# An attention and two-MLP kernel: two weight blocks are multiplied after the last attention products, and the sums for the second half of the tokens are made during the last two blocks of the first half

## The chip, the cores and the metric

The kernel runs on one core of one Trainium2 chip. A core has five engines that run their own instruction lists side by side: TensorE (PE in the profile, with its weight loads as PEld), VectorE (DVE), ScalarE (ACT), GpSimd (POOL) and SyncE (SP), which issues the DMA transfers. The metric is the time of one execution in microseconds (us); lower is better. A difference under about 0.3% (2.9 us here) can't be told from no change.

## The reference, cut to what matters

```python
def attention(q, k, v):                    # 4 batches x 8 heads x 576 positions x 64
    scores = (q @ k.T) / 8
    # heads 0-3 see the last 32 positions; heads 4-7 every 32nd earlier position
    p = softmax(where(mask, scores, -1e9))
    return p @ v
x = attention(q, k, v)                     # brought to 2304 tokens x 512
xn = x / sqrt(mean(x * x) + 1e-6) * rms_g
g = silu(xn @ w_gate) * (xn @ w_val)       # 512 -> 1536
x = g @ w_out                              # 1536 -> 512
x = softplus(x @ w_in) @ w_out2            # 512 -> 2048 -> 512
```

The weights arrive as 64-bit floats. The kernel turns them into 32-bit floats on the chip: one ScalarE and three VectorE instructions for each 128x512 piece (`decode`, L267).

## The kernel before, in words

**Precision.** Every matrix product of the MLPs is made of three products (`mm3`, L332; the matmul is L338): a number is split into a high part and a low part (ScalarE makes the high one; VectorE at L260 or GpSimd at L262 subtracts it to get the low one), and hi x hi, hi x lo and lo x hi are added in PSUM. The tile `win` holds split weights, `ob` and `tb` split activations, `gh`/`gl` the split hidden values, `xs` the activations.

**Tokens.** The 2304 tokens are cut into five chunks (512, 512, 512, 512, 256). Chunks 0 and 1 are side one (tokens 0 to 1023; batches 0 and 1 are tokens 0 to 1151), chunks 2, 3 and 4 are side two. The hidden width 1536 of the first MLP is cut into twelve blocks of 128, f = 0 to 11. A product of one block's gate or value rows with one 512-token chunk takes 12 matmuls; the text calls such a product a half (of the pair gate, value).

**Three stages, each planned as a whole.** The class `Program` (L49) records instructions and, at each `emit`, lists each engine's work in the order of a simulated schedule. TensorE has two streams (main work, and fillers marked `side`, which are taken where they can begin first); the other engines take what is ready by due times. Within an engine the order is fixed from then on.

1. *Attention of batches 0 and 1* (16 units; scores, mask, exponential, transposes, values), with fillers dealt to unit numbers by `at_step` (L861 to L869): weights of f = 0 and 1, the RMS statistics (`stats`, L344), normalising and splitting of chunk 0 at unit 13 and of chunk 1 at unit 20, that is after the last, and `half` and `glu` of f = 0 and 1 for chunk 0 from unit 14 to 19. `glu` loads ScalarE's silu table and then the exponential's again.
2. *Side one* of the first MLP, f = 0 to 11, with the attention of batches 2 and 3 dealt in, three items a pass; the items are used up at f = 9. Low parts of the hidden values (`chain1`, L724) are made on VectorE.
3. *The rest*: the remaining output products of side one (`drain`), `build` for side two, the first MLP on side two, then the second MLP on both sides.

**Side two and sums.** For two whole chunks `quad` makes a 2x2 block product with seven products in place of eight. It needs four sums of activations, T1 to T4, each split into high and low. `build` (L788) makes these and the plain splits at the start of side two, before the products that read them. `quad`'s results are put together with a ScalarE copy (L680) and a VectorE add (`plus`, L684). `early2` decodes weights of the second MLP, three pieces in each of the first blocks of side two.

**Output sums.** `out1` (first MLP) and `out2` (second) take PSUM into `xs`: the first block pair by a VectorE copy (L763, L781), the others by a VectorE add (L765, L783).

## Time and profile before

| | us |
|---|---|
| median of 3 runs | 967.75 (965.78 to 968.31) |
| profiled execution | 966.85 |
| its span in the trace | 964.8 |
| around the span | 2.05 |
| PE busy | 907.4 (94%) |
| DVE busy | 748.3 (78%) |
| ACT busy | 473.4 (49%) |
| POOL busy | 208.4 (22%) |

The profile is read by stretches of the span. Attention of batches 0 and 1 ends near 84 us, side one runs to 325 us, the first MLP on side two starts there. PE's busy share is near full in most stretches, and the granted clock stands beside it: at 0.50 TensorE runs at 1.2 GHz, at 1.00 at 2.4 GHz. A row of the timeline merges neighbouring instructions of one line; "[3.73 <-POOL ssq L566]" means that the engine had been idle for 3.73 us and was released by GpSimd's write of `ssq` at L566.

### The profile page before, as it was taken

The page shows a single profiled execution, that of the slowest core. Times are in us where ns is not written, and L with a number is a line of the kernel's source. Part 1 is how long each engine was busy: PE and PEld are TensorE (multiplying, and loading weights), DVE is VectorE, ACT ScalarE, POOL GpSimd, SP SyncE. Part 2 cuts the span into 40 slices and gives each one's busy share as a digit, 9 for nine tenths or more (in the row PEclk, how much of TensorE's full clock was granted, in tenths as well). Part 3 has the DMA queues.
Part 4 walks back from the last instruction along what each step waited for, and adds up shares of the span by engine and source line. Part 5 has one row for each costly group of instructions (what it writes and reads, how often), then busy time and mean ns, then how long its engine had stood idle before and what let it go on. Part 6 is the DMA issues. An engine that isn't in the chain of part 4 may idle for free.

```text
span 964.8 us, 14035 instructions
## 1 busy us (share of the span) xinstructions
PE 907.4 (94%) x5244; PEld 746.1 (77%) x5244; DVE 748.3 (78%) x1238; ACT 473.4 (49%) x883; POOL 208.4 (22%) x185
## 2 busy tenths in 40 slices
PE   6785999999999789999999988999999999999998
PEld 6663777777878667888888877888876888888886
DVE  6774879897943998999899997777779676666654
ACT  5576555556451545544445455444455544344331
POOL 2454111140222654332234161000013000000000
PEclk7777999999999889999999999999999999999999
DMA  9920966756420025545554422111120411101002
GB/s 196 257 76 25 280 201 188 228 135 189 140 88 1 22 88 153 175 142 176 164 168 149 151 68 55 55 45 48 53 65 22 153 40 38 44 23 44 22 1 109
DMA packets 42035, 103.11 MB, mean 107 GB/s; under 512 B 5040, under 2 KB 5744, under 8 KB 41968
## 3 DMA queue, kind: packets, MB, share of 16 engines
q1 hardware_dynamic: 41968, 102.23, 35.8%
q8 instruction: 41, 0.67, 0.3%
q14 instruction: 26, 0.21, 0.1%
HBM read 79.66 MB, written 22.54 MB: 106 GB/s over the span
## 4 chain that ended last, share of the span: by engine, by line
PE 46%; DVE 9%; DMA 2%; issue 2%; ACT 1%; POOL 0%; SPq 0%; ACTq 0%; DVEq 0%
PE bank L338 46%; DVE w L260 2%; DMA w<-w_kept 1%; DVE xs L765 1%; DVE xs L260 1%; DMA w_kept<-cvtx 1%; DVE cvu L277 1%; DVE win L260 1%; DVE cvu L275 1%; DVE gv L684 1%; DVE cvtx L280 0%; DVE gv L732 0%; ACT cvtx L274 0%; DVE gvx L684 0%; DVE tb L260 0%
## 5 line engine op out<-in xcount | busy, mean ns | idle before, releaser
L338 PE MATMUL bank<-ob,win 128*128 128x512 f32 (+1 forms) x1560 | 340.2, 364 | 10.8 <-ACT ob L255 5.2
L338 PEld LDWEIGHTS bank<-ob,win 128*128 128x128 f32 x1560 | 267.9, 192 | 62.3 <-ACT ob L255 6.7
L338 PE MATMUL bank<-tb,win 128*128 128x512 f32 x672 | 175.5, 396 | 13.6 <-ACT gv L680 5.8
L338 PEld LDWEIGHTS bank<-tb,win 128*128 128x128 f32 x672 | 126.0, 191 | 43.0 <-ACT gv L680 6.8
L783 DVE TENSOR_TENSOR xs<-bank,xs 128x512 f32<-128x512 f32 x126 | 86.5, 688 | 52.9 <-PE bank L338 52.5
L309 ACT ACTIVATE win<-w 128x512 fp32r<-128x512 f32 (+1 forms) x136 | 83.0, 614 | 86.9 <-DVE w L260 31.9
L338 PE MATMUL bank<-wout,ghx 128*128 128x512 f32 x304 | 94.1, 391 | 0.6 <-DVE xs L783 0.6
L260 DVE TENSOR_TENSOR win<-w,win 128x512 fp32r<-128x512 f32 x112 | 78.7, 703 | 19.7 <-ACT win L309 19.4
L338 PE MATMUL bank<-ghx,wout 128*128 128x512 f32 x224 | 84.9, 399 | 0.0
L338 PE MATMUL bank<-gh,wout 128*128 128x512 f32 (+1 forms) x256 | 81.8, 355 | 3.2 <-DVE xs L765 2.1
L338 PE MATMUL bank<-wout,gh 128*128 128x512 f32 x272 | 84.0, 390 | 0.0
L765 DVE TENSOR_TENSOR xs<-bank,xs 128x512 f32<-128x512 f32 (+1 forms) x100 | 62.3, 629 | 14.5 <-PE bank L338 14.1
L260 DVE TENSOR_TENSOR w<-w 128x256 f32<-128x256 f32 x112 | 71.1, 635 | 2.0
L338 PEld LDWEIGHTS bank<-wout,ghx 128*128 128x128 f32 x304 | 56.6, 188 | 13.3 <-DVE xs L783 1.9
L338 PE MATMUL bank<-wout,glx 128*128 128x512 f32 x152 | 59.3, 390 | 0.3 <-DVE glx L260 0.3
L338 PEld LDWEIGHTS bank<-wout,gh 128*128 128x128 f32 x272 | 50.8, 188 | 10.8 <-DVE xs L783 0.4
L338 PEld LDWEIGHTS bank<-gh,wout 128*128 128x128 f32 x256 | 45.8, 189 | 11.0 <-DVE xs L765 2.7
L277 DVE SCALAR_TENSOR_TENSOR cvu<-raw,cvu 128x512 uint32<-128x512 uint32 x68 | 52.3, 769 | 1.3
L338 PE MATMUL bank<-wout,gl 128*128 128x512 f32 x136 | 52.9, 389 | 0.0
L338 PEld LDWEIGHTS bank<-ghx,wout 128*128 128x128 f32 x224 | 42.1, 188 | 9.4 <-DVE xs L765 0.4
L720 ACT ACTIVATE gh<-gvx 128x512 fp32r<-128x512 f32 (+1 forms) x38 | 21.3, 561 | 56.0 <-PE bank L338 33.9
L338 PE MATMUL bank<-gl,wout 128*128 128x512 f32 (+1 forms) x128 | 44.9, 351 | 1.7 <-POOL gl L262 1.7
(153 smaller groups left out, 1381.8 us busy)
## 6 DMA issues: line engine op xcount, KB each, us to landing
raw<-w SPq DMA_DIRECT2D x68, 512.0 KB, 4.4
w<-w_kept SPq DMA_DIRECT2D x56, 256.0 KB, 2.6
w_kept<-cvtx SPq DMA_DIRECT2D x27, 256.0 KB, 4.4
cvt<-w_kept SPq DMA_DIRECT2D x27, 256.0 KB, 2.8
w_kept<-w SPq DMA_DIRECT2D x24, 256.0 KB, 3.9
out<-xs SPq DMA_DIRECT2D x18, 256.0 KB, 2.0
w_kept<-cvt SPq DMA_DIRECT2D x17, 256.0 KB, 4.6
cvtx<-w_kept SPq DMA_DIRECT2D x17, 256.0 KB, 3.0
```

The lines of the kernel that those rows point to most:

```text
L260: dve(n, lambda: getattr(nc.vector, name)(o, x, y), r, w)
L275: dve(512, lambda: nc.vector.tensor_scalar(out=u, in0=t.bitcast(U32), scalar1=0x80000000, scalar2=None, op0=ALU.bitwise_and), [kt], [ku], ...
L277: dve(512, lambda: nc.vector.scalar_tensor_tensor(out=u, in0=wlo, scalar=29, in1=u, op0=ALU.logical_shift_right, op1=ALU.bitwise_or), [kra ...
L309: act(n, lambda: nc.scalar.activation(h, t, AF.Copy), [kt], [reg(0, o + lo, o + hi)])
L338: lambda a=a, b=b, i=i, st=st, mv=mv: nc.tensor.matmul(o, lhsT=st[a], rhs=mv[b], start=(first and i == 0), stop=(last and i == m - 1), ski ...
L684: dve(CH, lambda: nc.vector.tensor_add(o[0], y[0], o[0]), [y[1], o[1]], [o[1]])
L720: act(n, lambda: nc.scalar.activation(h, src, AF.Copy), [ksrc], [kh])
L765: dve(n, lambda: nc.vector.tensor_add(x, pb, x), [kp, kx], [kx])
L783: dve(DM, lambda: nc.vector.tensor_add(x, pb, x), [kp, kx], [kx])
```

## The change

1. Chunk 1's statistics, normalising and splitting leave the fillers and come after attention, as do both `glu` of f = 0 and 1, which now share one silu table. The halves of f = 0 and 1 for chunk 0 go to fillers 18 and 19. The loads of their weights are planned behind the key loads of units 12 and 14 (`hold`). Chunk 1's low parts are all made on VectorE.
2. `sq`, which holds squares for the statistics, has two buffers in stage one.
3. The first `out1` and `out2` of a sum, copies out of PSUM, go from VectorE to ScalarE: 20 in the first MLP, 18 in the second.
4. f = 10 and 11 of side one go from stage two's plan to stage three's. There the low parts of their hidden values are made on GpSimd, and `combine`, the part of `build` that makes T1 to T4, stands behind f = 10. It writes its sums into the `gv` buffers, since chunks 2 and 3 are still read. `build` at the start of side two is left with the plain splits.
5. `early2`: two pieces a block for twelve blocks (24), and 8 more beside the second MLP's side one; before, three a block until 32 were made.

```diff
+DEALT = 10
-START = (13, 20)
+START = 14
+HOLD = (12, 14)
...
-        dma(512, lambda: nc.sync.dma_start(out=raw, in_=src), [], [kraw])
+        dma(512, lambda: nc.sync.dma_start(out=raw, in_=src), hold, [kraw])
...
-        sq = ring(at, "sq" + tag, 1, [128, 6 * SK])
+        sq = ring(at, "sq" + tag, nsq, [128, 6 * SK])
...
         if first:
-            dve(n, lambda: nc.vector.tensor_copy(x, pb), [kp], [kx])
+            act(n, lambda: nc.scalar.activation(x, pb, AF.Copy), [kp], [kx])
...
-    def build(c0, c1, c4, direct=True):
+    def combine(c0, c1, over):
         for k in (0, 1):
             (b11, k11), (b12, k12), (b21, k21), (b22, k22) = xv(k, c0), xv(k, c1), xv(k + 2, c0), xv(k + 2, c1)
-            if direct:
-                split_op(b11, k11, B11, k, eng="DVE")
-                split_op(b21, k21, B21, k, eng="DVE")
-                split_op(b22, k22, B22, k, eng="POOL")
             t, kt = fk["gv"].next()
             sub("DVE", CH, t, b12, b11, [k12, k11], [kt])
             split_op(t, kt, T1, k, eng="POOL")
             sub("POOL", CH, b12, b22, b12, [k22, k12], [k12])
             split_op(b12, k12, T3, k, eng="POOL")
-            two("DVE", CH, "tensor_add", b11, b12, b11, [k12, k11], [k11])
-            split_op(b11, k11, T2, k, eng="DVE")
-            sub("DVE", CH, b21, b21, b11, [k21, k11], [k21])
-            split_op(b21, k21, T4, k, eng="DVE")
+            t, kt = (b11, k11) if over else fk["gv"].next()
+            two("DVE", CH, "tensor_add", t, b12, b11, [k12, k11], [kt])
+            split_op(t, kt, T2, k, eng="DVE")
+            y, ky = (b21, k21) if over else fk["gv"].next()
+            sub("DVE", CH, y, b21, t, [k21, kt], [ky])
+            split_op(y, ky, T4, k, eng="DVE")
+    def build(c0, c1, c4, sums=True):
+        for k in (0, 1):
+            for kk, c, slot, eng in ((k, c0, B11, "DVE"), (k + 2, c0, B21, "DVE"), (k + 2, c1, B22, "POOL")):
+                x, kx = xv(kk, c)
+                split_op(x, kx, slot, k, eng=eng)
+        if sums:
+            combine(c0, c1, True)
...
-                split_op(x, kx, slots[kk // 2], kk % 2, eng="DVE" if kk % 2 else "POOL")
+                split_op(x, kx, slots[kk // 2], kk % 2, eng="DVE" if kk % 2 or c and kk < 3 else "POOL")
...
-        at_step(4, prep1, 0, 0)
-        at_step(9, prep1, 1, 0, (0,))
-        for c, u in enumerate(START):
-            at_step(u, stats, c, f_banks)
-            at_step(u, direct, c)
-        for f, u in ((0, START[0] + 1), (1, START[0] + 4)):
-            at_step(u, half, f, 0)
-            at_step(u + 1, half, f, 1)
-            at_step(u + 2, glu, f)
+        at_step(16, prepare, 0, (0, 1), HOLD[0])
+        at_step(17, prepare, 1, (0,), HOLD[1])
+        at_step(START, stats, 0, f_banks)
+        at_step(START, direct, 0)
+        for f, r_ in ((0, f_banks), (1, s_banks)):
+            for row in (0, 1):
+                at_step(18 + f, half, f, row, r_)
...
+            stats(1, t_banks)
+            direct(1)
+            table("silu_and_others")
+            for f in (0, 1):
+                g[f, 0] = chain1(gates[f, 0], gates[f, 1])
             pr.emit()
...
-            for f in range(W1N):
+            for f in range(DEALT):
+                side_a(f, queue)
             step(queue, len(queue))
             pr.emit(start=0)
...
+        for f in range(DEALT, W1N):
+            side_a(f, [])
+            if f == DEALT:
+                combine(*SIDES[1][:2], False)
         drain(len(todo))
-        build(*SIDES[1])
+        o_banks.t = banks.t[4:]
+        build(*SIDES[1], False)
...
-            for k in range(3 * f, min(3 * f + 3, 2 * W2N)):
-                early2(k)
+            early2(2 * f)
+            early2(2 * f + 1)
```

`side_a(f, queue)` is the loop body of stage two under a name: weights, gate and value products, `chain1` (its low parts on VectorE for f below 10, on GpSimd from there), and the output products to drain.

**TensorE at the end of stage one.** Rows of the order before: L526 are value products (`vb_105` of units 12 and 13, `vb_106` of the last two), L502 transposes, L338 halves, and L352, a few rows further on, the statistics of chunk 1.

```order
69 L338 MATMUL bank_76<-ob,win_89 128x512 x12
70 L338 MATMUL bank_77<-ob,win_89 128x512 x5
71 L526 MATMUL bank_75<-pt_115,vb_105 64x64 x6
72 L338 MATMUL bank_77<-ob,win_89 128x512 x2
73 L526 MATMUL bank_75<-pt_116,vb_105 64x64 x2
74 L502 MATMUL bank_72<-id_sb,pp_114 128x128 x3
75 L502 MATMUL bank_73<-id_sb,pp_114 128x128 x3
76 L338 MATMUL bank_77<-ob,win_89 128x512 x5
77 L338 MATMUL bank_76<-ob,win_89 128x512 x2
78 L526 MATMUL bank_74<-pt_117,vb_106 64x54 x6
```

The same place now; lines L530, L506, L342 and L356 are what L526, L502, L338 and L352 were.

```order
67 L530 MATMUL bank_75<-pt_115,vb_105 64x64 x6
68 L530 MATMUL bank_75<-pt_116,vb_105 64x64 x2
69 L342 MATMUL bank_77<-ob,win_89 128x512 x12
70 L342 MATMUL bank_76<-ob,win_89 128x512 x12
71 L342 MATMUL bank_70<-ob,win_89 128x512 x3
72 L506 MATMUL bank_72<-id_sb,pp_114 128x128 x3
73 L506 MATMUL bank_73<-id_sb,pp_114 128x128 x3
74 L342 MATMUL bank_70<-ob,win_89 128x512 x2
75 L530 MATMUL bank_74<-pt_117,vb_106 64x54 x6
76 L530 MATMUL bank_74<-pt_118,vb_106 64x54 x6
77 L530 MATMUL bank_75<-pt_117,vb_106 64x54 x6
78 L530 MATMUL bank_75<-pt_118,vb_106 64x54 x4
```

The value products of unit 13 (rows 67 and 68) stand ahead of 27 matmuls of halves now; before, 17 and more stood ahead of them. Between the last transposes and the value products of the last units stand two matmuls of halves, and none between those products; before, seven stood ahead of them and seven more between them.

**VectorE between stage two and stage three.** Before: L260 are low parts of weights (`win`) and of hidden values (`glx`), L356 to L359 the statistics of chunks 3 and 4, L765 output sums.

```order
396 L260 TENSOR_TENSOR win_89<-w_82,win_89 128x512
397 L732 TENSOR_TENSOR gvx_916<-bank_77,gvx_916 128x512
398 L260 TENSOR_TENSOR win_89<-w_82,win_89 128x512
399 L260 TENSOR_TENSOR glx_923<-gvx_916,ghx_920 128x512
400 L356 SCALAR_TENSOR_TENSOR gvx_917<-bank_73,ssq_b 128x512
401 L356 SCALAR_TENSOR_TENSOR gv_83<-bank_72,ssq_b 128x256
402 L358 TENSOR_TENSOR gvx_917<-gvx_917,ssq_b 128x512
403 L358 TENSOR_TENSOR gv_83<-gv_83,ssq_b 128x256
404 L359 SCALAR_TENSOR_TENSOR ssq_b<-gvx_917,ssq_b 128x512
```

Now: L360 to L363 are the statistics, L279, L281 and L284 a decode of weights of f = 10, L262 low parts and sums.

```order
372 L362 TENSOR_TENSOR gv_83<-gv_83,ssq_b 128x256
373 L363 SCALAR_TENSOR_TENSOR ssq_b<-gvx_915,ssq_b 128x512
374 L363 SCALAR_TENSOR_TENSOR ssq_b<-gv_83,ssq_b 128x256
375 L279 TENSOR_SCALAR cvu_81<-w_82 128x512
376 L281 SCALAR_TENSOR_TENSOR cvu_81<-raw_78,cvu_81 128x512
377 L262 TENSOR_TENSOR gvx_915<-xs 128x512
378 L284 SCALAR_TENSOR_TENSOR w_82<-w_82,cvu_81 128x512
379 L279 TENSOR_SCALAR cvu_81<-w_82 128x512
380 L281 SCALAR_TENSOR_TENSOR cvu_81<-raw_79,cvu_81 128x512
381 L262 TENSOR_TENSOR win_89<-w_82,win_89 128x512
```

Before, the weights of f = 10 are decoded and split (rows 396 and 398 end it) ahead of the statistics of chunks 3 and 4; now their decode stands behind them, with `combine`'s first sum (377) in its middle. On TensorE the gate product of f = 10 follows the products of these statistics directly in both orders.

## Rows read from the trace of the kernel before

**Rows 1.** The page: the chain that ended last, by engine.
```profile
PE 46%; DVE 9%; DMA 2%; issue 2%; ACT 1%; POOL 0%; SPq 0%; ACTq 0%; DVEq 0%
```
**Rows 2.** Windows: stretch, length, busy time (instructions) of each engine; columns in row one.
```profile
core 0: us, PE busy (x) PEld busy (x) DVE busy (x) ACT busy (x) POOL busy (x), PEclk, DMA share, GB/s
282.00:325.00 43.00, 43.00 (x192) 35.56 (x191) 22.50 (x34) 14.21 (x27) 12.65 (x11) 1.00 0.02 7
325.00:374.00 49.00, 38.67 (x173) 30.90 (x172) 47.62 (x60) 25.32 (x47) 30.59 (x22) 0.90 0.28 86
336.00:340.00 4.00, 4.00 (x15) 3.20 (x15) 4.00 (x5) 2.13 (x4) 4.00 (x4) 0.61 0.01 2
440.00:560.00 120.00, 118.90 (x630) 102.38 (x629) 112.37 (x181) 59.20 (x108) 36.49 (x29) 1.00 0.49 156
...
600.00:620.00 20.00, 20.00 (x89) 16.55 (x89) 15.45 (x26) 9.74 (x18) 0.00 (x0) 1.00 0.22 62
```
**Rows 3.** Timeline, end of stage one: start, busy, engine, line, operation, [idle before <-releaser].
```profile
42.51 1.87 PE L445 MATMUL bank<-kl,ql 128*64 128x96 f32 x20 [2.23 <-DVE eb L458]
...
66.42 1.32 POOL L485 TENSOR_TENSOR pp<-eb,mz 128x324 f32<-128x324 f32 x2 [1.27 <-DVE mz L476]
66.69 6.09 PE L338 MATMUL bank<-ob,win 128*128 128x512 f32 x20
...
74.14 0.87 PE L502 MATMUL bank<-id_sb,pp 128*128 128x128 f32 x6
...
79.12 1.28 ACT L198 ACT_TABLE_LOAD   x1
79.23 0.79 PE L526 MATMUL bank<-pt,vb 54*64 54x54 f32 x20
...
82.67 1.26 POOL L262 TENSOR_TENSOR gl<-gv,gh 128x512 fp32r<-128x512 f32 x1
...
84.64 2.08 PE L352 MATMUL bank<-ssq,ones 128*128 128x512 f32 x2 [3.73 <-POOL ssq L566]
```
**Rows 4.** VectorE by line, 36 to 49 us: count | busy us, mean ns | idle before.
```profile
L277 DVE SCALAR_TENSOR_TENSOR cvu<-raw,cvu 128x512 uint32<-128x512 uint32 x2 | 2.0, 1024 | 0.0
L280 DVE SCALAR_TENSOR_TENSOR w<-w,cvu 128x512 uint32<-128x512 uint32 x2 | 1.9, 956 | 0.0
L260 DVE TENSOR_TENSOR win<-w,win 128x512 fp32r<-128x512 f32 x2 | 1.8, 883 | 0.0
```
**Rows 5.** Timeline, the statistics of chunks 3 and 4.
```profile
280.50 1.56 PE L352 MATMUL bank<-ssq_b,ones 128*128 128x512 f32 x4 [0.64 <-POOL ssq_b L566]
...
281.70 3.10 PE L338 MATMUL bank<-ob,win 128*128 128x512 f32 x12
...
283.73 1.28 ACT L198 ACT_TABLE_LOAD   x1
...
286.12 8.45 POOL L262 TENSOR_TENSOR xs<-xs,ssq_b 128x512 f32<-128x512 f32 x8 [5.68 <-DVE ssq_b L359]
...
286.81 0.87 DVE L359 SCALAR_TENSOR_TENSOR ssq_b<-gv,ssq_b 128x256 f32<-128x256 f32 x1
```
**Rows 6.** Waits of PE, 325 to 380 us: total, times, longest.
```profile
PE bank L338 <- POOL tb L262: 4.2, 1, 4.2
```
**Rows 7.** Timeline, PE and DVE, the start of side two.
```profile
325.44 1.52 PE L338 MATMUL bank<-ob,win 128*128 128x512 f32 x6
...
333.89 1.76 DVE L260 TENSOR_TENSOR ob<-xs,ob 128x512 fp32r<-128x512 f32 x1
335.58 0.68 DVE L765 TENSOR_TENSOR xs<-bank,xs 128x512 f32<-128x512 f32 x1
...
370.88 1.52 PE L338 MATMUL bank<-tb,win 128*128 128x512 f32 x6
372.24 1.59 PE L338 MATMUL bank<-ob,win 128*128 128x256 f32 x12
372.57 0.68 DVE L684 TENSOR_TENSOR gvx<-bank,gvx 128x512 f32<-128x512 f32 x1
```

More of the change, by code (lines that the diff above doesn't have):

```diff
@@ L265, in sub @@
         two(eng, n, "tensor_sub", o, x, y, r, w)
+    hold = []
     def decode(src, t, kt, keep):
@@ L423, in load @@
                 dma((y1 - y0) / 2, lambda y0=y0, y1=y1: nc.sync.dma_start(
-                    out=kt[0:64, :, y0:y1], in_=src[:, :, y0:y1]), [], [(kk, a0, a1)])
+                    out=kt[0:64, :, y0:y1], in_=src[:, :, y0:y1]), [], [(kk, a0, a1), ("load" + tag, u // 2, u // 2 + 1)])
         def load_v(u):
@@ L780, in out2 @@
         if first:
[L781 removed]
+            act(DM, lambda: nc.scalar.activation(x, pb, AF.Copy), [kp], [kx])
         else:
@@ L848, in direct, with half, prepare @@
                 x, kx = xview(kk, CUTS[c], CUTS[c + 1])
-                split_op(x, kx, slots[kk // 2], kk % 2, eng="DVE" if kk % 2 else "POOL")
-        first = {}
-        def half(f, row):
-            first[f, row] = plain(w_at(f, 0), row, 0, f_banks)
-        def glu(f):
-            table("silu_and_others")
-            g[f, 0] = chain1(first[f, 0], first[f, 1])
-            table(EXP_LN)
-        at_step(4, prep1, 0, 0)
-        at_step(9, prep1, 1, 0, (0,))
-        for c, u in enumerate(START):
-            at_step(u, stats, c, f_banks)
-            at_step(u, direct, c)
-        for f, u in ((0, START[0] + 1), (1, START[0] + 4)):
-            at_step(u, half, f, 0)
-            at_step(u + 1, half, f, 1)
-            at_step(u + 2, glu, f)
+                split_op(x, kx, slots[kk // 2], kk % 2, eng="DVE" if kk % 2 or c and kk < 3 else "POOL")
+        gates = {}
+        def half(f, row, ring_):
+            gates[f, row] = plain(w_at(f, 0), row, 0, ring_)
+        def prepare(f, parts, u):
+            hold.append(("load", u // 2, u // 2 + 1))
+            prep1(f, 0, parts)
+            hold.clear()
+        at_step(16, prepare, 0, (0, 1), HOLD[0])
[5 more added lines that the diff above has]
+                at_step(18 + f, half, f, row, r_)
         def fill(u):
@@ L896, in outs1, with side_a @@
             return [(out1, [f - 1, f], g, first, c, d) for c in cs for d in range(KD)]
+        def side_a(f, queue):
+            if f:
+                prep1(f, 0, (0, 1) if f > 1 else (1,))
+            w = w_at(f, 0)
+            for c in (0, 1) if f > 1 else (1,):
+                gate = plain(w, 0, c, f_banks)
+                step(queue)
+                drain(1)
+                val = plain(w, 1, c, f_banks)
+                step(queue)
+                g[f, c] = chain1(gate, val, eng="DVE" if f < DEALT else "POOL")
+                drain(1 if f < W1N - 1 else 0)
+                step(queue)
+            if f % 2:
+                todo.extend(outs1(f, f == 1, (0, 1)))
         with ExitStack() as c2:
@@ L900, in attn_glu_softplus @@
             tv = Ring(banks.t[2:4], "bank", 2)
-            x = attention(at2, "b", (2, 3), 1, 2, 3, Ring(banks.t[:2], "bank", 0), tv, tv)
+            x = attention(at2, "b", (2, 3), 1, 2, 3, 1, Ring(banks.t[:2], "bank", 0), tv, tv)
             x.fixed(0)
-            table("silu_and_others")
             queue = steps(x, {1: (2,)}, tv)
             o_banks.t = banks.t[4:6]
-            for f in range(W1N):
-                if f:
-                    prep1(f, 0, (0, 1) if f > 1 else (1,))
-                w = w_at(f, 0)
-                for c in (0, 1) if f > 1 else (1,):
-                    gate = plain(w, 0, c, f_banks)
-                    step(queue)
-                    drain(1)
-                    val = plain(w, 1, c, f_banks)
-                    step(queue)
-                    g[f, c] = chain1(gate, val, eng="DVE")
-                    drain(1 if f < W1N - 1 else 0)
-                    step(queue)
-                if f % 2:
-                    todo.extend(outs1(f, f == 1, (0, 1)))
+            for f in range(DEALT):
+                side_a(f, queue)
             step(queue, len(queue))
             pr.emit(start=0)
-        o_banks.t = banks.t[4:]
+        o_banks.t = banks.t[4:6] + banks.t[2:4]
         wc = ctx.enter_context(tc.tile_pool(name="wc", bufs=1))
@@ L961, in attn_glu_softplus @@
                 i = prep2(p, c4 is not None)
+                if side == 0 and p < 4:
+                    early2(2 * W1N + 2 * p)
+                    early2(2 * W1N + 2 * p + 1)
                 def gap(k):
```

9 lines of the change are left out of this document (4 added, 5 removed).

## The prediction

> **What bounds the kernel now.** I read the chain of waits by engine first. TensorE carries 46% of the chain, VectorE 9%, and the rest little [rows 1]. The windows show where TensorE is not full. From 282 to 325 us and from 600 to 620 us it is busy all the time; from 440 to 560 it lacks 1.1 of 120 us; from 325 to 374, the start of side two, it lacks 10.3 of 49 us and its granted clock is 0.90, while VectorE is busy for 47.62 of 49 [rows 2]. So the kernel is bound by TensorE, except at the end of attention and at the start of side two. The change edits both places. The timelines give what ends the waits there [rows 3, 5, 7]. Below, S stands for the start of the statistics product of chunks 3 and 4, in the kernel before 280.50 [rows 5].
>
> **Part 1, the end of attention.** Everything after it waits for the statistics of chunk 1, whose product starts at 84.64 after 3.73 us of idle TensorE, released by GpSimd's sum of squares [rows 3]. Three things move it.
>
> - Weights of f = 0 and 1 leave VectorE's list between 36 and 49 us. Three groups of their instructions take 2.0, 1.9 and 1.8 us there [rows 4]. Attention waits for VectorE in that stretch: TensorE stands for 2.23 us at 42.51 [rows 3]. The gain lies between 2.2 and 5.7 us; I take 4. But the same work comes back between 50 and 70 us, 5.7 us and a little more, say 6.5. The last probabilities `pp`, done at 66.42 + 1.32 = 67.74, are then ready at about 67.7 - 4 + 6.5 = 70.2.
> - Before, these probabilities lie for 6.4 us: their transposes start at 74.14, since TensorE does matmuls of halves first, 20 of them in 6.09 us [rows 3]. By the order shown the halves now stand elsewhere or fit into the wait for `pp`. Transposes at about 70.4; from the transposes to the last value products it was 79.23 - 74.14 = 5.1 us, with 14 matmuls of halves between, and it should now be 3.4, with two. The last value product starts near 73.8 in place of 79.23: 5.4 us.
> - From the end of the last value products (79.23 + 0.79 = 80.02) to the statistics it was 4.6 us. In it lay a table load of 1.28 us on ScalarE and a low part of 1.26 us on GpSimd, which the sums of squares queue behind [rows 3]. Both now stand after the statistics: 2.5 us.
>
> The sum is 7.9, taken as 8. The displaced ten matmuls of halves run beside the chain that follows the statistics, where TensorE is idle in any case; the silu, product and split of these halves follow on engines that wait there too. I count them at nothing, and at 2 us if they get in front of the normalising. If the held weights land late, the halves come late, and the gain goes down to 3; at most it is 12, if the weights cost nothing between 50 and 70.
>
> **Part 2, the border to f = 10.** Here the change adds a wait. Before, the gate product of f = 10 starts 1.2 us after S, at 281.70, since its weights are split [rows 5]. Now, by VectorE's order, they are decoded behind the statistics. The statistics end with 286.81 + 0.87 = 287.68, 7.2 us after S [rows 5]; by the order an output sum (0.68 in [rows 7]) stood among them that is gone now, so some 6.4. ScalarE's first step of the decode waits for the silu table, which is loaded at 283.73 + 1.28, 4.5 us after S [rows 5], so it is no later. Behind that stand three VectorE instructions, `combine`'s first sum, whose inputs GpSimd is still normalising (8 in 8.45 us from 286.12 [rows 5]), a high part on ScalarE, and a low part. With 1.0 us an instruction on average this is 6 us: gate weights at S + 12.4. TensorE is free at S + 1.6, so the bubble is 10.8 us. Its ends are 8, with every VectorE instruction at the 0.68 of [rows 7], and 13. Queued behind the gate product on TensorE are all the output products and the value product, so nothing fills the bubble. After a shorter wait of 4.2 us [rows 6] the granted clock was 0.61 in the window 336 to 340 [rows 2], so TensorE ran some 4 us near the 1.2 GHz level; I add 3 us, between 1 and 5.
>
> **Part 3, the start of side two.** From 281.70 the two blocks f = 10 and 11 take until 325.44: 43.7 us at full rate, with VectorE half idle (22.50 of 43) [rows 2, 5, 7]. From 325.44 the first three blocks of side two take until 372.24 + 1.43 = 373.67: 48.2 us. At full rate this is 18 groups of six 512-column matmuls at 372.24 - 370.88 = 1.36 and five groups of twelve 256-column ones at 1.43: 31.6. So 16.6 us are lost there, 4.2 of it in one wait for the sums `tb` [rows 6]. That is what making T1 to T4 beside f = 10 can win at most.
>
> What is late next is VectorE: it is full in this stretch, and its work moves into the blocks before rather than going away. Counted in the order of the changed kernel, 107 VectorE instructions stand between S + 15 (behind the first weights of f = 10) and the last `plus` of f = 2 in side two. One takes 15.45/26 = 0.59 with GpSimd idle and 47.62/60 = 0.79 with GpSimd busy for 30.59 of 49 [rows 2]. GpSimd's work of both stretches, 12.65 + 30.59 = 43 us [rows 2], spreads over some 92: a share of 0.47, which lies between 0 and 0.62 so that a VectorE instruction costs 0.59 + 0.20 x 0.47/0.62 = 0.74. So that add comes at S + 15 + 107 x 0.74 = S + 94.2, against 372.57 - 280.50 = S + 92.1 before: 2 us later. TensorE's own sum is 10.8 + 3 + 43.7 + 31.6 + 2 (small waits that remain) = 91.1 against 373.67 - 281.70 = 92.0. The later of the two decides: I take +2.5, between -6 (bubble at its low end, VectorE at 0.66) and +13 (VectorE at 0.84). The gain of part 3 pays for the bubble of part 2, no more.
>
> The row that decides is VectorE's price beside GpSimd: an instruction with both inputs in SBUF took 1.76 us at 333.89 with GpSimd busy, one with an input in PSUM 0.68 at 335.58 [rows 7]. The Trainium skill (SBUF — State Buffer, "Who interferes with whom") says that VectorE with two SBUF inputs contends with a GpSimd instruction that reads SBUF, that one engine blocks the other fully, and that VectorE with at most one SBUF input doesn't contend. The two rows agree with it. By that rule the work moved to GpSimd (the low parts of f = 10 and 11, `combine`) is paid for on VectorE as well; that is the first rival.
>
> **Part 4, the rest.** In the first MLP on side two, 8 decodes fewer of three VectorE instructions (1.8 us each at 0.59) and 12 copies moved to ScalarE (59.20 of 120 busy) relieve VectorE, which was busy 112.37 of 120; TensorE lacks 1.1 us there [rows 2], so -1. The eight decodes return in the second MLP's side one: 14 us of VectorE, which had 4.5 us free in each 20 [rows 2]. Cover is there for most, but not beside the sums at its start: +1, between -1 and +4. The second buffer of `sq` and the all-VectorE split of chunk 1 (two low parts more on VectorE, two fewer on GpSimd) count as nothing: inside part 1's bounds.
>
> **Sum.** -8 + 2.5 - 1 + 1 = -5.5 us. The profiled execution took 966.85, so 961.35; it lay 0.90 under the median of 967.75, on whose level the time is 962.2, and I say 962.
>
> **Rivals.**
> 1. *VectorE becomes the bound through GpSimd (slower).* Place: S + 15 to the end of f = 2. Price: each 0.01 us in the mean VectorE instruction costs 1.07 us. At a mean of 0.79 (what it was at the start of side two) the whole gain is gone; from about 0.82 the kernel is slower by more than 0.3%. At 0.84 the stretch costs 2 + 10.7 = +12.7, and the time is 967.75 - 8 + 12.7 = 972.5. For it: 1.76 against 0.68 [rows 7]. Against it: 22.50/34 = 0.66 in 282 to 325 with GpSimd at work [rows 2].
> 2. *VectorE has slack and side two starts without a stall.* Bubble 9.5, clock 1.5, then 43.7 + 31.6 = 86.3 against 92.0: -5.7. With -8, -1 and +0.5 it is -14.2, 953.5. For it: VectorE idle for 20 of 43 us in f = 10 and 11 [rows 2]. Against: it must first make up the bubble.
> 3. *The end of attention doesn't move.* The decode in 50 to 70 us delays `pp` by what the halves delayed it before; -2 in place of -8: 968.2, the change not doing what it says. For it: the chain to `pp` goes through VectorE (1.27 us of wait for `mz` at 66.42 [rows 3]). Against: 6.4 us of `pp` lying idle.
>
> **How the numbers follow.** Forecast 0.40 (its own range 957 to 966), rival 1 0.23, rival 2 0.22, rival 3 0.15. A measurement of this kernel tells about 0.3% from no change, so faster means below 964.85 and slower above 970.65. Faster: 0.31 of the forecast, 0.21 of rival 2, 0.01 of rival 3 = 0.53. Slower: 0.19 of rival 1, 0.03 of rival 3, 0.02 of the forecast = 0.24. Same: 0.23. The range 952 to 973 takes in rivals 1 and 2 to their middles.
>
> **What the profile after would show.** Part 1: the statistics product of chunk 1 near 76.7 with the transposes directly behind `pp`; if it starts above 82, rival 3. Part 2: an idle time of 8 to 13 us ahead of the gate product of f = 10, ended by a low part of `win`, with the granted clock near 0.5 behind it; if it is under 5, the order misled me. Part 3: no wait for `tb` over 1 us, and the mean VectorE instruction from there to f = 2: 0.74, above 0.82 for rival 1, under 0.68 for rival 2. Part 4: TensorE still full from 440 to 560 on the old clock of the span. A loss over 4 us in the second MLP's side one would make the sum wrong where I looked least.

## The result: 1% slower, and where the time went

The changed kernel took 977.09 us (median of 4 runs, 976.64 to 978.48), the kernel before 968.03 beside it: a ratio of 1.0099, interval 1.0079 to 1.0120. The profiled execution took 977.51 us, its span 975.7. Forecast were 962 and a range of 952 to 973.

The span is best read between landmarks on TensorE, each the start of a row of its timeline: the statistics product of chunk 1; S, that of chunks 3 and 4; side two's first product; the last 256-column group of f = 2 of side two (the fifth such group from there); the second MLP's first product. Lengths in us; the runs E1 to E12 are told below. Each row is one execution. The last column repeats to 0.4 us from E6 to E11, but the start varies more: the statistics of chunk 1 come at 75.7 to 78.4 with the new stage one, and at 84.64 and 82.14 with the old one (before and E4).

| | to stat. 1 | to S | to side two | to f = 2 | to MLP 2 | to the end | span |
|---|---|---|---|---|---|---|---|
| before | 84.64 | 195.86 | 44.94 | 46.80 | 209.91 | 382.65 | 964.8 |
| after | 76.65 | 202.90 | 67.81 | 33.12 | 211.07 | 384.15 | 975.7 |
| E1 f = 10 early | 75.66 | 202.33 | 56.25 | 35.06 | 211.04 | 387.06 | 967.4 |
| E2 lows on VectorE | 77.52 | 201.47 | 66.72 | 34.25 | 211.06 | 386.98 | 978.0 |
| E3 no dealing | 77.16 | 200.17 | 44.96 | 43.02 | 213.76 | 387.03 | 966.1 |
| E4 old stage one | 82.14 | 195.88 | 65.50 | 33.44 | 211.04 | 385.50 | 973.5 |
| E5 both early | 75.87 | 201.84 | 53.95 | 34.24 | 212.33 | 385.47 | 963.7 |
| E6 E3, old decodes | 77.80 | 200.47 | 44.95 | 46.81 | 215.43 | 382.94 | 968.4 |
| E7 E5, old decodes | 76.71 | 203.31 | 52.51 | 33.68 | 216.30 | 382.59 | 965.1 |
| E8 E7, `wout` on GpSimd | 77.92 | 202.41 | 54.80 | 31.63 | 215.59 | 382.65 | 965.0 |
| E9 E7, copies on VectorE | 76.51 | 200.34 | 53.90 | 32.94 | 217.18 | 382.63 | 963.5 |
| E10 E9, masks first | 78.41 | 200.07 | 54.09 | 32.90 | 217.16 | 382.67 | 965.3 |
| E11 stage one alone | 76.34 | 200.28 | 44.96 | 46.86 | 209.70 | 382.66 | 960.8 |
| E12 E5, normalising moved | 77.48 | 200.46 | 54.38 | 33.91 | 211.10 | 384.17 | 961.5 |

After against before: -8.0, +7.0, +22.9, -13.7, +1.2, +1.5, in all +10.9.

**The end of attention** came as forecast (the timeline after; lines L356, L449 and L342 answer to L352, L445 and L338 of [rows 3]).

```profile
76.65 1.12 PE L356 MATMUL bank<-ssq,ones 128*128 128x512 f32 x2
...
98.40 0.67 ACT L278 ACTIVATE w<-raw 128x512 f32<-128x512 f32 x1 [3.13 <-DMA raw<-w]
...
99.10 0.43 DVE L279 TENSOR_SCALAR cvu<-w 128x512 uint32<-128x512 uint32 x1 [1.40 <-ACT w L278]
...
101.04 0.69 DVE L262 TENSOR_TENSOR wout<-cvtx,wout 128x512 fp32r<-128x512 f32 x1 [1.51 <-ACT wout L333]
...
103.32 0.55 DVE L462 TENSOR_TENSOR ebb<-bank,mzb 128x384 f32<-128x384 f32 x1
...
103.92 0.79 PE L449 MATMUL bank<-ksb,qsb 128*64 128x54 f32 x20 [2.27 <-DVE ebb L462]
...
111.01 5.49 PE L342 MATMUL bank<-ob,win 128*128 128x512 f32 x12 [3.34 <-ACT gv L735]
```

Row one is 8.0 us earlier than before. The other rows are the start of side one. VectorE stands twice, at a decode whose data ScalarE has only just got from the DMA (99.10) and at a low part (101.04), with the mask of attention's second tile (103.32) behind both. So TensorE waits 2.27 us for that mask, then 3.34 for a silu that stands on ScalarE behind the exponentials, and its next twelve matmuls take 5.49 us. The same places in the timeline before, and behind them the first output product of both kernels:

```profile
106.02 0.66 ACT L274 ACTIVATE w<-raw 128x512 f32<-128x512 f32 x1 [3.01 <-DMA raw<-w]
...
107.05 0.55 DVE L458 TENSOR_TENSOR ebb<-bank,mzb 128x384 f32<-128x384 f32 x1
...
113.83 3.03 PE L338 MATMUL bank<-ob,win 128*128 128x512 f32 x12 [1.44 <-ACT gv L731]
...
116.70 0.39 PE L338 MATMUL bank<-gh,wout 128*128 128x512 f32 x1
```
```profile
116.30 0.50 PE L342 MATMUL bank<-gh,wout 128*128 128x512 f32 x1
```

The first output product starts at 116.3, before at 116.7: the lead is gone. That is where every run with the new stage one loses it. From the statistics of chunk 1 to the first output product it is 32.0 and 32.1 us with the old stage one (E4 and before) and 37.1 to 39.8 in every run with the new one; from there to S it is 162.9 to 163.9 us in all fourteen.

**The border to f = 10** (timeline after, answering to [rows 5]).

```profile
279.55 1.56 PE L356 MATMUL bank<-ssq_b,ones 128*128 128x512 f32 x4 [0.78 <-POOL ssq_b L570]
...
285.18 10.31 POOL L264 TENSOR_TENSOR xs<-xs,ssq_b 128x512 f32<-128x512 f32 x8 [5.68 <-DVE ssq_b L363]
285.29 1.49 DVE L279 TENSOR_SCALAR cvu<-w 128x512 uint32<-128x512 uint32 x1
286.81 1.63 DVE L281 SCALAR_TENSOR_TENSOR cvu<-raw,cvu 128x512 uint32<-128x512 uint32 x1
288.37 1.74 DVE L262 TENSOR_TENSOR gvx<-xs 128x512 f32<-128x512 f32 x1
...
290.03 1.75 DVE L284 SCALAR_TENSOR_TENSOR w<-w,cvu 128x512 uint32<-128x512 uint32 x1
...
292.50 1.22 PE L342 MATMUL bank<-ob,win 128*128 128x512 f32 x2 [11.39 <-ACT win L313]
...
294.96 4.63 PE L342 MATMUL bank<-ob,win 128*128 128x512 f32 x10 [1.25 <-DVE win L262]
```

The decode stands behind the statistics, with `combine`'s first sum in it, and GpSimd normalises beside all of it. The gate product starts at S + 12.95, where S + 12.4 was forecast; it was S + 1.2 before.

**The end of f = 11** (timeline after): the last low part of side one is on GpSimd, behind the splits for side two.

```profile
334.04 0.63 ACT L313 ACTIVATE win<-w 128x512 fp32r<-128x512 f32 x1 [4.89 <-DVE w L262]
...
334.57 0.58 ACT L735 ACTIVATE gvx<-bank 128x512 f32<-128x512 f32 x1
...
336.25 2.12 POOL L264 TENSOR_TENSOR ob<-xs,ob 128x256 fp32r<-128x256 f32 x3
...
336.53 0.50 PE L342 MATMUL bank<-gh,wout 128*128 128x512 f32 x1 [0.76 <-DVE xs L769]
...
337.32 0.61 ACT L724 ACTIVATE ghx<-gvx 128x512 fp32r<-128x512 f32 x1
...
337.99 0.50 PE L342 MATMUL bank<-ghx,wout 128*128 128x512 f32 x1 [0.49 <-ACT ghx L724]
...
338.32 1.27 POOL L264 TENSOR_TENSOR win<-w,win 128x512 fp32r<-128x512 f32 x1
...
339.55 1.44 POOL L264 TENSOR_TENSOR glx<-gvx,ghx 128x512 fp32r<-128x512 f32 x1
...
341.05 0.50 PE L342 MATMUL bank<-glx,wout 128*128 128x512 f32 x1 [2.56 <-POOL glx L264]
...
341.89 0.63 PE L342 MATMUL bank<-gl,wout 128*128 128x512 f32 x1
```

The waits are 3.8 us, and the last row shows a matmul of 0.63 in place of 0.39: the lower clock behind them. The last hidden value is late from its silu on (334.57), although TensorE had ended its products by 330.3. ScalarE had stood idle for 4.89 us ahead of it, at a high part of side two's weights that waited for a sum on VectorE (334.04). Behind the silu, the high part `ghx` (337.32) and GpSimd's low part `glx` (339.55) each stand behind work for side two in their engine's list.

**Windows after**, columns as in [rows 2]:

```profile
284.00:292.00 8.00, 0.00 (x0) 0.00 (x0) 7.86 (x9) 2.12 (x5) 6.82 (x5) 0.50 0.19 66
292.00:347.00 55.00, 49.44 (x191) 38.89 (x192) 49.62 (x69) 25.06 (x46) 28.20 (x22) 0.89 0.42 129
342.00:345.00 3.00, 3.00 (x9) 2.33 (x8) 3.00 (x6) 0.63 (x1) 3.00 (x3) 0.50 0.31 93
347.00:382.00 35.00, 33.46 (x172) 27.68 (x171) 29.98 (x46) 19.91 (x38) 14.43 (x12) 1.00 0.48 151
294.55:382.00 87.45, 81.68 (x359) 66.07 (x360) 77.09 (x111) 44.52 (x82) 40.08 (x31) 0.94 0.45 139
440.00:560.00 120.00, 118.83 (x625) 101.34 (x625) 96.81 (x156) 56.37 (x102) 37.97 (x28) 1.00 0.38 122
```

The first row is the bubble: TensorE does nothing, VectorE is busy 7.86 of 8 us. The second is f = 10 and 11, 55 us for 43.7 us of products, at a clock of 0.89; the third is the low clock at its end. In the fourth, side two starts almost without idle time. The fifth runs from S + 15 to f = 2 of side two: VectorE takes 77.09/111 = 0.69 us an instruction there and is idle for 10.4 of 87.45 us. In the sixth VectorE has 15.6 us less to do than in [rows 2], and TensorE is as full as it was.

### The profile page after: what moved, and what is told of

Same layout as the page of the kernel before. It is cut to its first block, busy times and chain, and to the rows that moved or that the text cites. A ratio compares the mean times of both kernels' runs of the same rounds, so it can differ in the third digit from the quotient of the medians.

```text
span 975.7 us, 14001 instructions
## 1 busy us (share of the span) xinstructions
PE 908.3 (93%) x5244; PEld 746.2 (76%) x5244; DVE 723.5 (74%) x1198; ACT 489.0 (50%) x917; POOL 213.2 (22%) x187
## 4 chain that ended last, share of the span: by engine, by line
PE 77%; DVE 15%; issue 3%; ACT 3%; DMA 2%; POOL 0%; SPq 0%; DVEq 0%; ACTq 0%; POOLq 0%
PE bank L342 71%; PE bank L449 3%; DVE xs L262 2%; PE bank L530 2%; DVE w L262 2%; PE bank L506 1%; DVE xs L769 1%; DVE cvu L281 1%; DVE win L262 1%; DVE cvu L279 1%; DVE ob L262 1%; DVE tb L262 1%; DMA ql<-q_t 1%; DVE gvx L262 1%; DVE gv L688 1%
## 5 line engine op out<-in xcount | busy, mean ns | idle before, releaser
L342 PE MATMUL bank<-ob,win 128*128 128x512 f32 (+1 forms) x1560 | 343.6, 367 | 26.0 <-ACT win L313 11.4
L342 PEld LDWEIGHTS bank<-ob,win 128*128 128x128 f32 x1560 | 270.0, 193 | 78.4 <-ACT win L313 11.8
L342 PE MATMUL bank<-tb,win 128*128 128x512 f32 x672 | 172.7, 392 | 7.8 <-ACT gvx L684 3.6
L342 PEld LDWEIGHTS bank<-tb,win 128*128 128x128 f32 x672 | 124.1, 188 | 37.1 <-ACT gv L684 5.0
L313 ACT ACTIVATE win<-w 128x512 fp32r<-128x512 f32 (+1 forms) x136 | 83.2, 615 | 77.8 <-DVE w L262 34.6
L262 DVE TENSOR_TENSOR win<-w,win 128x512 fp32r<-128x512 f32 x112 | 80.0, 715 | 22.3 <-ACT win L313 22.0
L342 PE MATMUL bank<-wout,ghx 128*128 128x512 f32 x304 | 94.0, 391 | 0.6 <-DVE xs L787 0.5
L342 PE MATMUL bank<-ghx,wout 128*128 128x512 f32 x224 | 86.0, 403 | 0.5 <-ACT ghx L724 0.5
L342 PE MATMUL bank<-gh,wout 128*128 128x512 f32 (+1 forms) x256 | 83.1, 362 | 3.0 <-DVE xs L769 2.9
L342 PE MATMUL bank<-wout,gh 128*128 128x512 f32 x272 | 84.0, 390 | 0.0
L262 DVE TENSOR_TENSOR w<-w 128x256 f32<-128x256 f32 x112 | 65.9, 588 | 1.3
L342 PEld LDWEIGHTS bank<-wout,ghx 128*128 128x128 f32 x304 | 56.6, 188 | 13.2 <-DVE xs L787 1.8
L342 PE MATMUL bank<-wout,glx 128*128 128x512 f32 x152 | 59.3, 390 | 0.3 <-DVE glx L262 0.3
L342 PEld LDWEIGHTS bank<-wout,gh 128*128 128x128 f32 x272 | 50.8, 188 | 10.8 <-DVE xs L787 0.4
L281 DVE SCALAR_TENSOR_TENSOR cvu<-raw,cvu 128x512 uint32<-128x512 uint32 x68 | 56.6, 833 | 1.3
L342 PEld LDWEIGHTS bank<-gh,wout 128*128 128x128 f32 x256 | 46.9, 194 | 11.4 <-DVE xs L769 4.3
L342 PE MATMUL bank<-wout,gl 128*128 128x512 f32 x136 | 52.9, 389 | 0.0
L342 PEld LDWEIGHTS bank<-ghx,wout 128*128 128x128 f32 x224 | 43.1, 192 | 10.3 <-ACT ghx L724 0.9
L688 DVE TENSOR_TENSOR gv<-bank,gv 128x512 f32<-128x512 f32 x48 | 33.0, 687 | 20.5 <-ACT gv L684 14.1
L342 PE MATMUL bank<-gl,wout 128*128 128x512 f32 (+1 forms) x128 | 46.2, 361 | 1.7 <-POOL gl L264 1.7
```

The lines of the kernel that those rows point to most:

```text
L262: dve(n, lambda: getattr(nc.vector, name)(o, x, y), r, w)
L281: dve(512, lambda: nc.vector.scalar_tensor_tensor(out=u, in0=wlo, scalar=29, in1=u, op0=ALU.logical_shift_right, op1=ALU.bitwise_or), [kra ...
L313: act(n, lambda: nc.scalar.activation(h, t, AF.Copy), [kt], [reg(0, o + lo, o + hi)])
L342: lambda a=a, b=b, i=i, st=st, mv=mv: nc.tensor.matmul(o, lhsT=st[a], rhs=mv[b], start=(first and i == 0), stop=(last and i == m - 1), ski ...
L688: dve(CH, lambda: nc.vector.tensor_add(o[0], y[0], o[0]), [y[1], o[1]], [o[1]])
```

## The experiments

Each ratio is to the kernel before, run on the same chip. Every edit is to the changed kernel; where a run builds on another (E6 on E3, E7 and E12 on E5, E8 and E9 on E7, E10 on E9), the edits of that one belong to it, and the code shows what is added.

**E1, f = 10's weights early.** 969.19 us, ratio 1.0013 (0.9998 to 1.0028).

```diff
-            if f:
+            if f and f != DEALT:
                 prep1(f, 0, (0, 1) if f > 1 else (1,))
...
             for f in range(DEALT):
                 side_a(f, queue)
+            prep1(DEALT, 0)
```

> The changed kernel, with the weights of f = 10 (its first preparation) recorded in stage two, behind f = 9, so that their decode and split stand ahead of the statistics of chunks 3 and 4 on VectorE. Theory (a bubble of TensorE at the border): the 12.6 us of idle time ahead of and in the first gate product of f = 10 and about 3.4 us of low clock behind it go, -16 us: about 961 us, gate product 1.2 us after the statistics product. Rival (VectorE beside GpSimd is the bound from f = 10 to f = 2): the same VectorE work stands there, so at most -5 us, about 972, with TensorE waiting for VectorE further on instead.

The bubble is gone (gate product at S + 1.2), and the kernel is 8 us faster than the changed one: between the two expectations, nearer the rival's. Its waits from 300 us on, and its window from 279 to 334:

```profile
PE bank L342 <- DVE xs L769: 4.1, 2, 2.7
PE bank L342 <- DVE gv L736: 3.8, 1, 3.8
PE bank L342 <- ACT tb L257: 2.1, 1, 2.1
```
```profile
279.00:334.00 55.00, 46.96 (x194) 36.84 (x193) 52.30 (x64) 26.36 (x47) 36.89 (x26) 0.97 0.26 82
```

TensorE now waits most for VectorE, which is busy 52.30 of 55 us, 0.82 an instruction. The bubble was real, and VectorE was next behind it: the stretch to side two is 56.25, not 45.

**E2, low parts of f = 10 and 11 on VectorE.** 978.20 us, 1.0100 (1.0073 to 1.0127).

```diff
-                g[f, c] = chain1(gate, val, eng="DVE" if f < DEALT else "POOL")
+                g[f, c] = chain1(gate, val, eng="DVE")
```

> The changed kernel, with the low parts of the hidden values of f = 10 and 11 made on VectorE, as for the other blocks. Theory (the last output products of f = 11 wait for GpSimd's queue): the 2.56 us wait for the low part of f = 11 and the low clock behind it go, some -6 us: about 971 us. Rival (VectorE is the bound there): four more VectorE instructions in the stretch, +2 to +3 us or no gain: 977 to 980.

The theory fell: the wait for GpSimd's low part is gone, but TensorE waits at the same place for an output sum:

```profile
PE bank L342 <- DVE xs L769: 2.9, 1, 2.9
```

The end of f = 11 is not GpSimd's queue alone: the silu of the last hidden value starts earlier here (331.95), but VectorE multiplies it only at 336.05, behind two steps of a decode (1.79 and 1.10 us) that stand ahead of it in its list.

**E3, no dealing: f = 10 and 11 and the sums where they were.** 968.20 us, 1.0006 (0.9991 to 1.0021).

```diff
-DEALT = 10
+DEALT = W1N
...
-        build(*SIDES[1], False)
+        build(*SIDES[1])
```

> The changed kernel, with f = 10 and 11 back in stage two's plan and the sums T1 to T4 made at the start of side two, as before; parts 1, 2, 3 and 5 of the change stay. Theory: the border wait, the wait at the end of f = 11 and the gain at the start of side two all go, and with it all of the loss but the 2.7 us that came behind side two's first blocks: 967 to 970 us, with the 8 us of the end of attention not showing. Rival (the gain at the end of attention is real and only the border hides it): 960 us.

As the theory had it. (All instructions are there, but the changed kernel also has another ring of four PSUM banks for output products, `banks.t[4:6] + banks.t[2:4]`, and by the code some output sums of side one are overwritten with this ring and this order; E6 and E11 use the ring of before.) The dealing with the early sums costs 977.1 - 968.2 = 9 us.

**E4, stage one as before.** 976.79 us, 1.0088 (1.0066 to 1.0111).

```diff
-START = 14
-HOLD = (12, 14)
+START = (13, 20)
...
+        at_step(4, prep1, 0, 0)
+        at_step(9, prep1, 1, 0, (0,))
+        for c, u in enumerate(START):
+            at_step(u, stats, c, f_banks)
+            at_step(u, direct, c)
...
+            at_step(u + 2, glu, f)
```

> The changed kernel, with stage one as before (statistics of chunk 1 and both silu steps among the fillers, weights of f = 0 and 1 at units 4 and 9, one buffer of squares); parts 3, 4 and 5 stay. Theory (the 8 us won at the end of attention are given back in the first 25 us of side one): about +1, 976 to 979 us, with the statistics product of chunks 3 and 4 near 280.5. Rival (they are kept): +8, 985 us.

The theory holds: with the old stage one the way from statistics 1 to S is 195.88, with the new one 200.1 to 203.3 in every run. S comes at 278.02, 1.5 us earlier than in the changed kernel, and the two times (ratios 1.0088 and 1.0099) are not told apart.

**E5, weights of f = 10 and 11 early.** 967.14 us, 1.0000 (0.9979 to 1.0020).

```diff
             for f in range(DEALT):
                 side_a(f, queue)
+            for f in range(DEALT, W1N):
+                prep1(f, 0)
```

> The changed kernel, with the weights of f = 10 and of f = 11 recorded in stage two, so that the decode and most splits of both stand ahead of the statistics of chunks 3 and 4. In the run with f = 10 alone TensorE still lost some 8 us between the statistics and side two, waiting for VectorE, which was busy 52.3 of 55 us. Theory (what is left is VectorE's load in this stretch): some ten instructions of 0.7 to 1.7 us leave it, TensorE's waits there fall under 3 us, 961 to 964 us. Rival (GpSimd's work slows whatever VectorE does there, mean 0.82 us, so the loss stays): 967 to 970 us.

The time is the rival's, but not for its reason: VectorE's mean from 279 to 332 us is 47.37/62 = 0.76, not 0.82. It is still 53.95 to side two, and E5 is not told from E1 (ratios 1.0000 and 1.0013, with intervals that overlap). TensorE's longest waits in the stretch:

```profile
311.48 3.03 PE L342 MATMUL bank<-ob,win 128*128 128x512 f32 x12 [2.26 <-DVE gv L736]
320.98 0.50 PE L342 MATMUL bank<-gh,wout 128*128 128x512 f32 x1 [1.03 <-DVE xs L769]
324.22 0.80 PE L342 MATMUL bank<-glx,wout 128*128 128x512 f32 x1 [2.05 <-POOL glx L264]
```

**E6, no dealing, decodes of the second MLP's weights as before.** 970.29 us, 1.0034 (1.0013 to 1.0055).

```diff
-            early2(2 * f)
-            early2(2 * f + 1)
+            for k in range(3 * f, min(3 * f + 3, 2 * W2N)):
+                early2(k)
```

> The changed kernel, with f = 10 and 11 back in stage two and the sums at the start of side two (output products of side one in the four banks as before), and with the second MLP's weights decoded three pieces a block in the first MLP and none beside the second. Parts 1, 2 and 3 stay. Theory (the loss behind side two's first blocks comes from the eight decodes at the start of the second MLP: a wait of 2.28 us and low clock behind it): 963 to 966 us, and no wait over 1 us there. Rival (it comes from the copies that ScalarE makes now): 968 us, with the 2.28 us wait in place.

Half of the theory: the second MLP takes 382.94 again (384 to 387 with the spread decodes), and the wait at its start is 1.03 us in place of 2.28. But the stretches before it got longer by more: 46.81 to f = 2 and 215.43 from there, in E3 43.02 and 213.76.

**E7, E5 with the old decodes.** 966.37 us, 0.9983 (0.9961 to 1.0004).

```diff
+            for f in range(DEALT, W1N):
+                prep1(f, 0)
...
-                if side == 0 and p < 4:
-                    early2(2 * W1N + 2 * p)
-                    early2(2 * W1N + 2 * p + 1)
```

> The changed kernel with both blocks' weights recorded in stage two and the second MLP's weights decoded as before. Theory: the two gains add, 3 to 5 us under the run with both blocks' weights early alone, 957 to 960 us. Rival (three decodes a block delay the first MLP on side two, whose first blocks are VectorE's): no more than 1 us under it.

The rival: what the second MLP gives back (-2.9), the first MLP on side two loses (+4.0).

**E8, E7 with f = 1's output weights' low part on GpSimd.** 966.12 us, 0.9977 (0.9961 to 0.9994).

```diff
-        sub("DVE", 512, w[:, 1], t, w[:, 0].bitcast(F32), [kt, (kw, 0, 512)], [(kw, 512, 1024)])
+        sub("POOL" if keep == 5 else "DVE", 512, w[:, 1], t, w[:, 0].bitcast(F32), [kt, (kw, 0, 512)], [(kw, 512, 1024)])
```

> As the run before it, and the low part of f = 1's output weights, which stands ahead of attention's masking on VectorE at the start of side one and waits there for ScalarE, is made on GpSimd. Theory (VectorE's order behind that wait gives back the lead of attention): TensorE's waits of 2.3 and 3.3 us before 112 us shrink, from the statistics of chunk 1 to those of chunks 3 and 4 it is 197 us or less in place of 200 to 203, and the time is 3 to 5 us lower, 953 to 957. Rival (the landing of the data and the exponential's table set it): no change within 1 us.

The rival: 202.41 to S. With that instruction gone the mask still stands behind decode steps on VectorE, one of which (L284, at 102.86) takes 1.67 us while GpSimd makes the low part; TensorE's two waits are 1.91 and 3.05 us, in E7 2.33 and 3.35.

**E9, E7 with the copies on VectorE.** 967.60 us, 1.0013 (0.9998 to 1.0028).

```diff
-            act(n, lambda: nc.scalar.activation(x, pb, AF.Copy), [kp], [kx])
+            dve(n, lambda: nc.vector.tensor_copy(x, pb), [kp], [kx])
```

> Weights of f = 10 and 11 in stage two, the second MLP's weights decoded as before, and the first copies out of PSUM on VectorE again, as before the change; stage one, the dealing and the early sums stay. In the runs with these copies on ScalarE and the decodes as before, from the last product of f = 2 of side two to the second MLP took 215.4 to 216.3 us, against 209.9 in the kernel before. Theory (the copies on ScalarE delay its other work in the first MLP on side two): that stretch goes back to 210 to 211 us, and the time is 960 to 963. Rival (the copies are a relief of VectorE and something else is late there): 966 us or more.

The theory fell: 217.18 to the second MLP. With the sums made early the copies are not what is late there.

**E10, E9 with f = 2's decode behind the masks.** 966.18 us, 0.9984 (0.9967 to 1.0000).

```diff
-        act(512, lambda: nc.scalar.activation(t, whi.bitcast(F32), AF.Copy, scale=2.0 ** -112), [kraw], [kt])
+        act(512, lambda: nc.scalar.activation(t, whi.bitcast(F32), AF.Copy, scale=2.0 ** -112), [kraw] + after, [kt])
...
+            if f == 2:
+                after.append(("ebb1", 0, 1 << 20))
```

> As the run before it, and the plan holds the decode of f = 2's weights behind the second mask of side one's first attention unit, so that VectorE's list has that unit's masks first and the decode, whose data land late, behind them. Theory (the lead of attention is given back since VectorE and ScalarE stand in order at a decode whose data are still on the way, with the masks behind it): the waits of TensorE of 2 to 3 us before 112 us go, from the statistics of chunk 1 to those of chunks 3 and 4 it is 194 to 198 us in place of 200 to 203, and the time is 3 to 6 us lower, 955 to 959. Rival (the lead is lost to something that sets the pace of side one whatever the order): the same stretch and no change over 1 us.

The two waits are gone, and another stands in their place, since the weights are decoded later (from 106.65 on, in E9 from 98.21):

```profile
106.65 0.66 ACT L278 ACTIVATE w<-raw 128x512 f32<-128x512 f32 x1
...
110.67 0.74 PE L342 MATMUL bank<-ob,win 128*128 128x512 f32 x2 [4.49 <-ACT win L313]
```

200.07 us to S, as with the other order (E9: 200.34). The medians are 1.4 us apart, and the intervals of the two ratios just touch (0.9967 to 1.0000 and 0.9998 to 1.0028), which is at the edge of what can be told, and less than the 3 to 6 us of the theory.

**E11, stage one's change alone.** 964.31 us, 0.9971 (0.9959 to 0.9984). E6 with the copies on VectorE: the edits shown at E3, E6 and E9 together, with the ring of banks of before:

```diff
-DEALT = 10
+DEALT = W1N
...
-        o_banks.t = banks.t[4:6] + banks.t[2:4]
+        o_banks.t = banks.t[4:]
```

> The kernel before with stage one of the changed kernel and nothing else of it: f = 10 and 11 in stage two, sums at the start of side two, copies on VectorE, decodes of the second MLP's weights as before. Theory (won at the end of attention, given back in side one): statistics of chunk 1 near 76.7 us, those of chunks 3 and 4 at 278 to 280, and 965 to 968 us, within 0.3% of before. Rival (the gain of 8 us shows once the rest is undone): 960 us.

Between the two: 2.8 us faster than before, the best of all versions, and just about what can be told from no change. Of the 8 us at the statistics, 4.4 are lost by S.

**E12, E5 with the normalising of chunks 3 and 4 on VectorE.** 967.07 us, 0.9998 (0.9983 to 1.0012).

```diff
-                norm(c, "POOL")
+                norm(c, "DVE" if c > 2 else "POOL")
```

> The changed kernel with the weights of f = 10 and 11 in stage two (as in the run with both blocks early), and the normalising of chunks 3 and 4, 8 products that took GpSimd 9.88 us there, on VectorE. Theory (GpSimd's work stretches VectorE's beside it: instructions that take 0.68 us alone took 1.2 to 1.8): VectorE gets 4.4 us more work but loses some 6 us of stretching, and the sums start earlier; from the statistics to side two 48 to 51 us in place of 54.0, 963 to 965 us. Rival (VectorE's load alone counts): 4 us more in that stretch, 968 to 971 us.

The eight products, in E5 on GpSimd and in E12 on VectorE, and of each run `combine`'s first sum behind them (`gvx<-xs`, two inputs in SBUF) and of E5 an output sum (one input in PSUM):

```profile
283.35 9.88 POOL L264 TENSOR_TENSOR xs<-xs,ssq_b 128x512 f32<-128x512 f32 x8 [5.69 <-DVE ssq_b L363]
283.46 0.68 DVE L769 TENSOR_TENSOR xs<-bank,xs 128x512 f32<-128x512 f32 x1
...
286.59 1.77 DVE L262 TENSOR_TENSOR gvx<-xs 128x512 f32<-128x512 f32 x1
```
```profile
283.68 3.83 DVE L262 TENSOR_TENSOR xs<-xs,ssq_b 128x512 f32<-128x512 f32 x8
...
288.62 0.68 DVE L262 TENSOR_TENSOR gvx<-xs 128x512 f32<-128x512 f32 x1
```

VectorE does them in 3.83 us, and the sum behind them takes 0.68 us, where it took 1.77 beside GpSimd's products. The Trainium skill (SBUF — State Buffer, "Who interferes with whom") has it that a VectorE instruction with two SBUF inputs contends with a GpSimd instruction that reads SBUF, and the rows agree with it. The prediction cited the section's other rule without its exception: with at most one SBUF input a VectorE instruction is free of this contention only outside the 2-port modes, which `tensor_scalar` can enter. The rows agree with that too: the decode step L279, a `TENSOR_SCALAR`, took 0.43 us at 99.10 and 1.49 beside GpSimd at 285.29.

Neither expectation came about. VectorE's busy time from 279 to 332 is 48.56 us for 68 instructions, in E5 47.37 for 62. Without the eight products that is 0.75 us an instruction against 0.76, so the stretching went at this place and hardly at all in the stretch. To side two it is 54.38, no less than in E5. What the stretching costs TensorE is therefore not shown.

## Why the prediction was wrong, by its own steps

| | forecast | measured |
|---|---|---|
| part 1, statistics of chunk 1 | -8 | -8.0 |
| from there to S | 0 | +7.0 |
| parts 2 and 3, S to f = 2 | +2.5 | +9.2 |
| part 4, the rest | 0 | +2.7 |
| sum | -5.5 | +10.9 |

Two steps failed: part 1's gain was carried to the end, and in part 3 the wait for the last hidden value of f = 11 was put at nothing.

- **Part 1 was right at its place, and wrong in that its gain was carried to the end.** The statistics came at 76.65, forecast 76.7. That it fits so well is luck in part: the transposes started at 71.72, forecast 70.4, since 23 matmuls of halves (7.58 us from 64.31) still stood ahead of them, and from there to the end of the value products it took 2.5 us, forecast 4.2. The step that failed is "Everything after it waits for the statistics of chunk 1": it was read as if side one would move with them. From E11 and the changed kernel against the one before, 4.4 to 7 of the 8 us are lost before S, and they are lost ahead of the first output product. Up to 2.5 us of that are TensorE's clock: behind the same wait of 3.3 us the next twelve matmuls took 5.49 us in the changed kernel, at a granted clock of 0.50, and 3.03 in E9, at 1.00. It isn't the landing of f = 2's first weights: ScalarE takes them 21.8 us behind the statistics (98.40), before 21.4 (106.02). But the second mask comes 26.7 us behind the statistics on VectorE (103.32), before 22.4 (107.05). E8 and E10 changed the order there and moved the wait, not the time; neither has the order of before, so whether that order would keep the lead stays open. A row that could have warned stood in the trace before: the decode and the masks were already mixed there (106.02 and 107.05).
- **Part 2's mechanism and size were right**: bubble forecast 10.8 us, measured 11.39, ended by a high part of `win`, and then 1.25 for the low part; clock forecast 3, measured 3.4 (18 matmuls from 292.50 took 8.95 us with 1.25 of wait in them, against 4.30 before). E1 shows it by taking it away.
- **Part 3 is the other step that failed.** TensorE's sum of 91.1 measured 100.8 (from the end of the statistics product, S + 1.6, to the end of f = 2). Of the 9.7 us more, 6.5 lie in the term of 43.7, which put f = 10 and 11 at their old full rate: 3.8 are the waits at 336 to 341 for an output sum and the last hidden value of f = 11, and 2.7 slower matmuls around and behind them, most at the low clock of 342 to 345. The forecast had no such wait beyond 2 us of small ones: it took two engines' sums and let the later decide, but the last hidden value passes ScalarE, VectorE, ScalarE and GpSimd in turn, and on ScalarE (twice) and GpSimd it stood behind work for side two in an in-order list, while TensorE had no other product to fill in. E2 shows that taking GpSimd out of that chain is not enough. The bubble was 1.8 us over its term, the clock behind it 0.4. Side two's blocks were nearly as forecast, 33.12 + 1.43 = 34.6 for 31.6 + 2.
- **VectorE's price was forecast too high, not too low**: 0.69 from S + 15 to f = 2, forecast 0.74. Yet the last `plus` of f = 2 came at S + 100.2 (379.75), forecast S + 94.2, with VectorE idle for 10.4 us on the way. So **rival 1** had the sign but not the mechanism: at 0.69 it should not have come about.
- **Even without the bubble the early sums win nothing.** From S to the second MLP it is 301.65 before and 300.52 in E5: to side two +9.0, from there -10.1. What the start of side two wins is paid in f = 10 and 11: in E5, too, TensorE waits there for hidden values and output sums (the three rows of E5). That an order exists which avoids these waits is neither shown nor excluded.
- **Part 4** was forecast as a swap worth nothing and costs 2.7, all behind f = 2. The spread decodes cost the second MLP 1.5 to 4.4 us (E1 to E5 and E12 against the rest), and the decodes as before cost the first MLP as much or more wherever the copies are on ScalarE or the sums early. By timing, copies and decodes together, with the ring of banks, are E3 less E11: 0.35%, 3.4 us, with 0.2% to either side. The copies by themselves cost 5.7 us without the dealing (E6 less E11 in the stretch to the second MLP) and nothing with it (E7 and E9); why they differ was not found.

By timing, undone one by one: the dealing +0.93% (after less E3), copies, decodes and ring +0.35% (E3 less E11), stage one -0.29% (E11 less before).

## What to carry to other kernels

A gain of time at one landmark is not a gain at the end until the next landmark has been looked at: put starts of the same instructions of both kernels side by side. Moving work ahead into a stretch where an engine looks half idle is free only if no value that the next stage waits for is made behind it in an in-order queue: the larger of two engines' sums does not show that (S + 94 forecast, S + 100 measured), the order of the lists does. When a block moves to another plan, leave its preparation in the old one if the new one would put it behind other work: that alone was worth 8 us here.
